# Block-recurrent cross attention and SwiGLU on one core: how weights are converted, and how batch 0 opens, dealt anew

## The chip, the core and the metric

The kernel runs on one core of a Trainium2 chip, in one launch. The metric is device time in microseconds (us). Engines are named as the profile names them: PE (TensorE; PEld are its weight loads), DVE (VectorE), ACT (ScalarE), POOL (GpSimd) and SP (SyncE), which issues most DMAs; ACT issues some.

## The reference

Eight batches of eight heads; each head has 512 tokens and 32 states of 64 features. Tokens attend to states and states to tokens; the two reads are stacked to 544 rows per batch, and the heads are laid side by side to 512 features. Then comes a feed-forward block with RMS norm and a gated hidden layer of 1536. The weights arrive as 64-bit floats, and there is no arithmetic on the host.

```python
scores = scale * np.matmul(x, state.transpose(0, 1, 3, 2))      # 512 x 32 per head
a = np.exp(scores - scores.max(-1, keepdims=True))
a /= a.sum(-1, keepdims=True) + 1e-09
xread = np.matmul(a, state)
...                                                              # a2: the same from states to tokens
sread = np.matmul(a2, x)
x = concat([xread, sread], axis=2) -> (4352, 512)
xn = x / np.sqrt(np.mean(x * x, axis=-1, keepdims=True) + 1e-06) * rms_g
g, val = xn @ w_gate, xn @ w_val                                 # 512 -> 1536
out = g * (1.0 / (1.0 + np.exp(-g))) * val @ w_out               # 1536 -> 512
```

## The kernel before

**The work.** A token's read is a mixture of states, so the gate and value weights are first multiplied with the batch's states (`own_weights`, L695, copied to SBUF at L707). A hidden product then takes the attention weights `aT_s` of the batch, scaled by each token's norm, straight to the hidden layer: `hidden` for batch 0 (products L738, Silu L744, gating L748), `hidden_seven` for the others (products L842). The output projection is `project_as_ready` for batch 0 (L945) and `project_twice` for the others (L1146). All products are in 32-bit floats.

**Stages.** Batch 0 is computed while the weights are loaded and converted, with batch 1's attention beside it. Its steps on PE, DVE, ACT, POOL and SP stand in the order that the string `ORDER` gives: every letter takes one step of one generator (`a`, `b`: the halves of batch 0's token attention; `A`: batch 1's; `s`, `S`: state reads; `e`, `d`: weight conversion on ACT and on DVE; `v`: own weights; `h`, `t`, `u`: hidden products, Silu, gating; `p`: projection; `z`: products of the identity matrix without use for the result, L1281). `FIRST` does the same for batch 1, `PERIOD` for batches 2 to 6, `LAST` for batch 7, `STATES` for the rows of the states. Each engine works through its own queue in that order.

**Weights.** A piece is 1 MB of 64-bit numbers, 128 rows by 1024. There are three for each of six pairs of hidden blocks (`mp`): 256 columns of `w_gate`, the same of `w_val`, and 256 rows of `w_out`. `load_parts` (L212) brings a piece into one of `RAW_AHEAD` = 4 buffers `raw`. `exponents` makes three passes over it on ACT (L246, L249, L252), which turn the top 16 bits into a power of two by rectifiers; `values` makes three on DVE: it masks the upper word (L273), joins the words to a mantissa (L276) and multiplies with the power (L282). The gate and value weights go to `w_m`, those of the output to `wo`; each finished `w_m` is also stored in DRAM, from where later batches fetch it.

**Batch 0's token attention.** `first_half` transposes the state rows (L463), copies them to `stT` (L466) and, with zeros between the heads, to `apart` (L468, L469). `chunk_scores` transposes 128 tokens of x at a time (L499, copied at L501) and multiplies them with `apart` (L504); maximum, difference and exponential follow (L510, L512, L514). `half_read` sums and normalizes (L522 to L527), transposes (L532, L535), multiplies with the states' Gram matrix (L539) and the weights again (L543), sums by products with ones (L548), takes the power -1/2 on POOL (`mean_root`, L299), spreads it along the rows (L306) and scales `aT_s` (L558). Each half has 256 tokens; the hidden products take all 512. `state_scores` (L568, copies L574) serves the state read.

## Time and profile before

| what | value |
|---|---|
| time before, three runs | 745.63 us median (742.44 to 745.95) |
| span of the profiled execution | 742.6 us; the page gives no time around it |
| PE busy | 735.6 us, 99% |
| DVE, ACT, POOL busy | 579.0, 380.2, 260.3 us |
| DMA | 146.15 MB, 197 GB/s over the span |
| ACT passes over a piece of 128x1024 (L246, L249, L252) | 1.25, 1.15, 1.15 us |
| DVE passes over a piece of 128x1024 (L273, L276, L282) | 0.68, 1.22, 1.22 us |

The page gives busy time by engine, a chain of work that ended last, and the costliest groups of instructions. A row of the timeline is: start in us, duration in us, engine, line, operation, what is written and read, shapes and count, and in brackets the idle time before it with what ended it. In the chain a row is start, duration, and engine with what it writes and the line. PE's records count a 32-bit product twice, as it is done in two passes.

### The profile page before, as it was taken

The page shows a single profiled execution, that of the slowest core. Times are in us where ns is not written, and L with a number is a line of the kernel's source. Part 1 is how long each engine was busy: PE and PEld are TensorE (multiplying, and loading weights), DVE is VectorE, ACT ScalarE, POOL GpSimd, SP SyncE. Part 2 cuts the span into 40 slices and gives each one's busy share as a digit, 9 for nine tenths or more (in the row PEclk, how much of TensorE's full clock was granted, in tenths as well). Part 3 has the DMA queues.
Part 4 walks back from the last instruction along what each step waited for, and adds up shares of the span by engine and source line. Part 5 has one row for each costly group of instructions (what it writes and reads, how often), then busy time and mean ns, then how long its engine had stood idle before and what let it go on. Part 6 is the DMA issues. An engine that isn't in the chain of part 4 may idle for free.

```text
span 742.6 us, 14225 instructions
## 1 busy us (share of the span) xinstructions
PE 735.6 (99%) x5582; PEld 591.0 (80%) x5582; DVE 579.0 (78%) x957; ACT 380.2 (51%) x635; POOL 260.3 (35%) x362
## 2 busy tenths in 40 slices
PE   8999999999999999999999999999999999999998
PEld 6534444779977998789878997799778987899996
DVE  4999978899856994699659985799469955798862
ACT  5999972573265725472366426562556336511220
POOL 3100004341283128512573228312841267324400
PEclk9999999999999999999999999999999999999999
DMA  9987936964783278608881669328860883063411
GB/s 296 274 294 274 398 118 223 309 245 148 239 304 105 90 285 283 195 1 297 228 304 23 226 213 315 98 95 292 274 188 6 317 230 127 1 223 117 135 52 28
DMA packets 60994, 146.15 MB, mean 197 GB/s; under 512 B 14848, under 2 KB 31744, under 8 KB 54016
## 3 DMA queue, kind: packets, MB, share of 16 engines
q1 hardware_dynamic: 47808, 125.78, 48.9%
q10 hardware_dynamic: 13120, 19.47, 9.2%
q8 instruction: 44, 0.72, 0.4%
q14 instruction: 22, 0.18, 0.1%
HBM read 116.46 MB, written 28.77 MB: 196 GB/s over the span
## 4 chain that ended last, share of the span: by engine, by line
PE 98%; ACT 1%; DMA 1%; DVE 0%; SPq 0%; issue 0%; DVEq 0%
PE f L842 40%; PE f L1146 31%; PE f L945 6%; PE pv L738 6%; PE pv L695 3%; PE at L695 3%; PE f L1008 2%; PE at L631 1%; PE at L355 1%; PE at L437 1%; DMA rows<-in_state_dram 1%; PE f L1281 0%; PE pv L504 0%; PE at L306 0%; PE at L499 0%; PE at L649 0%
## 5 line engine op out<-in xcount | busy, mean ns | idle before, releaser
L842 PE MATMUL f<-aT_s,v 128*128 128x256 f32 x504 | 118.8, 381 | 0.0
L842 PEld LDWEIGHTS f<-aT_s,v 128*128 128x128 f32 x504 | 94.8, 191 | 19.2 <-DVE h L1200 4.2
L905 DVE TENSOR_TENSOR g<-g,f 128x512 f32<-128x512 f32 x84 | 55.8, 684 | 58.6 <-PE f L842 45.7
L842 PE MATMUL f<-aT_t,vs 128*128 128x256 f32 x336 | 86.6, 381 | 0.0
L1174 POOL TENSOR_TENSOR kept<-kept 128x256 f32<-128x256 f32 x28 | 20.9, 746 | 183.2 <-DVE kept L1186 116.9
L1159 ACT COPY kept<-f 128x512 f32<-128x512 f32 (+1 forms) x56 | 30.1, 538 | 105.8 <-PE f L1146 99.8
L1146 PE MATMUL f<-w,h 128*128 128x128 f32 x588 | 74.7, 276 | 0.0
L842 PEld LDWEIGHTS f<-aT_t,vs 128*128 128x128 f32 x336 | 63.0, 190 | 12.5 <-issue 3.5
L1146 PEld LDWEIGHTS f<-w,h 128*128 128x128 f32 x588 | 69.8, 192 | 1.1 <-DVE h L1200 0.8
L722 POOL TENSOR_TENSOR vs<-v 128x256 f32<-128x256 f32 x42 | 31.0, 737 | 109.8 <-ACT v L707 109.6
L896 ACT ACTIVATE hb<-g 128x1024 f32<-128x1024 f32 x42 | 44.4, 1058 | 46.8 <-DVE g L905 43.1
L299 POOL TENSOR_TENSOR ri<-ss,mhalf 128x4 f32<-128x4 f32 (+1 forms) x9 | 9.4, 1045 | 126.9 <-issue 82.0
L918 DVE TENSOR_TENSOR hb<-hb,f 128x512 f32<-128x512 f32 (+1 forms) x48 | 31.1, 649 | 28.8 <-PE f L842 28.7
L945 PE MATMUL f<-wo,hb 128*128 128x512 f32 x96 | 44.0, 599 | 0.0
L738 PE MATMUL pv<-aT_s,v 128*128 128x512 f32 x96 | 43.8, 598 | 0.0
L842 PE MATMUL f<-aT_t,v 128*128 128x256 f32 x168 | 43.8, 383 | 0.0
L842 PE MATMUL f<-aT_s,vs 128*128 128x256 f32 x168 | 43.3, 380 | 0.0
L1146 PE MATMUL f<-wo,h 128*128 128x128 f32 x336 | 42.3, 275 | 0.0
L1146 PE MATMUL f<-wo,hb 128*128 128x128 f32 x336 | 42.1, 275 | 0.0
L918 DVE TENSOR_TENSOR hb<-hb,c 128x512 f32<-128x512 f32 (+1 forms) x48 | 35.7, 743 | 6.5 <-ACT hb L896 6.1
L1146 PEld LDWEIGHTS f<-wo,hb 128*128 128x128 f32 x336 | 40.3, 192 | 0.4
L1146 PEld LDWEIGHTS f<-wo,h 128*128 128x128 f32 x336 | 39.8, 192 | 0.0
(227 smaller groups left out, 1639.9 us busy)
## 6 DMA issues: line engine op xcount, KB each, us to landing
w_m<-w_d SPq DMA_DIRECT2D x48, 1024.0 KB
w<-t_d SPq DMA_DIRECT2D x49, 576.0 KB
out_dram<-kept SPq DMA_DIRECT2D x28, 256.0 KB
raw<-in_moe_w_val_dram SPq DMA_DIRECT2D x6, 1024.0 KB
raw<-in_moe_w_out_dram SPq DMA_DIRECT2D x6, 1024.0 KB
w_d<-w_m SPq DMA_DIRECT2D x6, 1024.0 KB
x_b<-in_x_dram SPq DMA_DIRECT2D x6, 1024.0 KB
x_d<-xB ACTq DMA_DIRECT2D x6, 1024.0 KB
```

What stands on the lines that cost most here:

```text
L695: TE.matmul(out=pv[e][Ns * j:Ns * j + Ns, :], lhsT=stT_g[b][D * e:D * e + D, j, :], rhs=w[D * e:D * e + D, j].rearrange("p m k f -> p (m k ...
L722: GE.tensor_tensor(out=vs[:, 0], in0=a21, in1=a22, op=ALU.add)
L738: TE.matmul(out=to[0], lhsT=lhs(i, k), rhs=r, start=(i == 0), stop=(i == len(rhs) - 1))
L842: TE.matmul(out=ps[:, i, 0:half], lhsT=l[:, i, :], rhs=r, start=(start and i == 0 and k == 0), stop=(k == len(lhs) - 1), skip_group_check= ...
L896: SE.activation(out=hb[:, 2 * mp:2 * mp + 2, 0:n].rearrange("p m (c t) -> p m c t", c=2), in_=q["g"][:, :, :, 0:half], func=ACTF.Silu if s ...
L905: VE.tensor_tensor(out=to, in0=to, in1=q[ps][:, :, 0:half], op=ALU.add)
L918: VE.tensor_tensor(out=part, in0=part, in1=val, op=ALU.mult)
L945: TE.matmul(out=banks[r], lhsT=hb[:, m, P * r:P * r + P], rhs=wo[:, m, :], start=(m == 0), stop=(m == NM - 1))
L1008: TE.matmul(out=banks[name][:, r, :], lhsT=lhs(k)[:, P * r:P * r + P], rhs=rhs(k), start=(start and r == 0 and k == 0), stop=(k == HM - 1) ...
L1146: TE.matmul(out=to[half][:, slot, :], lhsT=lhs[:, k, :], rhs=rhs[:, k, :], start=(fresh and n in (0, 4) and k == 0), stop=(k == QM - 1), s ...
L1159: SE.copy(of_half(k, i), banks[name][i])
L1174: GE.tensor_tensor(out=k[:, 4:8:3], in0=k[:, 5:6].to_broadcast([P, 2, QD]), in1=k[:, 4:8:3], op=ALU.add)
```

## The change

- **Conversion.** A piece lands two bytes off the start of its buffer, as 16-bit numbers, so that the 32 bits under the top 16 stand in one aligned word. ACT makes two rectifier passes (Prelu with slope 2^-20) that leave the top 16 bits as a bfloat16 number; DVE masks that to its power of two (16 bits in and out), multiplies the aligned word with it, and adds the bfloat16 number. `RAW_AHEAD` is 5. The first pair's gate and value pieces are cut by hidden block (128 columns of each) instead of by matrix.
- **Loads.** Batch 0's state rows come on ACT's queue, ahead of four rows of `rms_g`, which PE transposes. Batch 0's x comes on SP's queue in token halves (the first in two DMAs of four heads), with two neighbouring tokens side by side in runs of 512 bytes; the second half stands behind weight piece 0, and batch 1's x behind pieces 0 to 4.
- **Batch 0's attention in token halves.** One transpose covers two tokens of a head; scores use `apart` for either token. `half_read` transposes the unscaled exponentials, and one product with the Gram matrix and four columns of ones gives both the squares and the sums; the norm and the sum are then joined to one factor (with two small products and the power on POOL), the exponentials are scaled once and transposed again. The products by ones (L548), the spreading along the rows (L306) and the scaling of `aT_s` after it go.
- **Own weights and hidden products of the first pair** are made block by block (`first_own`) and by token half (`first_pair`), so that the first hidden products need half 0 and the first block alone.
- **Order.** `ORDER` and `FIRST` are written anew. The products without use take a matrix of ones set by DVE (`wake`); `z` does not occur in the new `ORDER`, and `y`, the same with other banks, occurs three times. The groups of POOL (L158, L160) move behind the opening as stream `i`; the Gram matrix and `stT_g` are a stream `g`. Memsets of `apart` and `blocks` move from POOL to DVE.
- Batch 0's token rows are stored in the new order of tokens, with as many DMAs.

```diff
-RAW_AHEAD = 4
+RAW_AHEAD = 5
 W_BUFS = 3
-FLAT = 1793.0
+FLAT = 2.0 ** 20
+ZERO = 16 * 896
...
-    "zzzaaazazbabaaabdebdbadeabeazszbbeadebeezdzbazzaabbaszeabbazzddbebeaaezbddabddsa"
+    "aaaaaaageeaaadadeeggbbigdddabbbaabgbaabgaeaaaayybydbebbvadbeeaabasvbbbvhssdbbedv"
...
+            rows[b] = x_0.tile([P, 3, D], F32, name="rows_0")
         for e in range(2):
-            nc.sync.dma_start(out=rows[b][:, e], in_=state[b, e::2])
-
-    def load_x(b, *queues):
+            (nc.sync if b else nc.scalar).dma_start(out=rows[b][:, e], in_=state[b, e::2])
...
+    def load_x_halves():
+
+        x_sb[0] = x_0.tile([P, 2, H, HT, D], F32, name="x_b")
+        for i in range(2):
+            for h in (slice(0, H // 2), slice(H // 2, H)) if i == 0 else (slice(0, H),):
+                nc.sync.dma_start(out=x_sb[0][:, i, h].rearrange("p h c d -> p h (c d)"),
+                                in_=x[0, h, HS * i:HS * i + HS, :].rearrange("h (p c) d -> p h (c d)", c=HT))
+            yield
+
+    wake = consts.tile([P, P], F32, name="wake")
+    VE.memset(wake, 1.0)
...
-    for i, bound in enumerate((-896.0 - 7.5 / 16, 1.0, 255.0 * 128, 1e-6)):
+    for i, bound in enumerate((-float(ZERO), 16.0 * ZERO / FLAT, 0.0, 1e-6)):
...
+    apart = x_0.tile([P, 2, 4, HT, Ns], F32, name="apart")
+    VE.memset(apart, 0.0)
     blocks = x_0.tile([P, P], F32, name="blocks")
-    GE.memset(blocks, 0.0)
+    VE.memset(blocks, 0.0)
+    gram = x_0.tile([P, 2, P + 4], F32, name="gram")
+    VE.memset(gram[:, :, P:P + 4], 0.0)
     for j in range(4):
-        GE.memset(blocks[Ns * j:Ns * j + Ns, Ns * j:Ns * j + Ns], 1.0 / DM)
+        VE.memset(blocks[Ns * j:Ns * j + Ns, Ns * j:Ns * j + Ns], 1.0 / DM)
+        VE.memset(gram[Ns * j:Ns * j + Ns, :, P + j:P + j + 1], 1.0)
...
+        for n in range(2):
+            if mp:
+                pieces.append([(moe_w_gate, moe_w_val)[n][:, 2 * P * mp:2 * P * mp + 2 * P]])
+            else:
+                pieces.append([dram[:, P * n:P * n + P] for dram in (moe_w_gate, moe_w_val)])
+        pieces.append([moe_w_out[2 * P * mp:2 * P * mp + 2 * P]])
...
+        raw[k] = raws.tile([P, 8 * P + 1, 4], I16, name="raw")
+        flat = raw[k].rearrange("p f four -> p (f four)")[:, 1:1 + 32 * P]
+        out_ = flat.rearrange("p (n f) -> p n f", n=len(pieces[k]))
+        for n, src in enumerate(pieces[k]):
+            nc.sync.dma_start(out=out_[:, n].rearrange("p (a f) -> p a f", a=src.shape[1]),
+                              in_=src.bitcast(I16))
...
-                ex, line = exs[k][:, columns(k, a)], lin[:, columns(k, a)]
-                half = raw[k][:, columns(k, a)].bitcast(I16)[:, :, 3::4]
-                SE.activation(out=line, in_=half, func=ACTF.Prelu, scale=1.0 / 16,
+                c = columns(k, a)
+                SE.activation(out=lin[:, c], in_=raw[k][:, c.start + 1:c.stop + 1, 0], func=ACTF.Prelu,
                               bias=bounds[:, 0:1], alpha=1.0 / FLAT)
                 yield
-                SE.activation(out=ex, in_=line, func=ACTF.Prelu, bias=bounds[:, 1:2],
-                              alpha=FLAT)
-                yield
-                SE.activation(out=ex.bitcast(U16), in_=ex, func=ACTF.Relu, scale=128.0,
-                              bias=bounds[:, 2:3])
+                SE.activation(out=tops[k][:, c], in_=lin[:, c], func=ACTF.Prelu, scale=8.0,
+                              bias=bounds[:, 1:2], alpha=FLAT)
...
+                        power_ = conv.tile([P, 8 * P], U16, name="power")
+                        words = raw[k].rearrange("p f four -> p (f four)").bitcast(U32)
+                        words = words[:, 0:16 * P].rearrange("p (f two) -> p f two", two=2)[:, :, 1]
...
-                    top, r = (t[:, columns(k, a)] for t in (top_, raw[k]))
-                    hi = r[:, :, 1]
-                    man = r.bitcast(F32)[:, :, 0]
-                    VE.tensor_scalar(top, hi, 0xfffff, 0x100000,
-                                     op0=ALU.bitwise_and, op1=ALU.bitwise_or)
+                    c = columns(k, a)
+                    top, power, rest = tops[k][:, c], power_[:, c], words[:, c].bitcast(F32)
+                    VE.tensor_scalar(power, top.bitcast(U16), 0xff80, None, op0=ALU.bitwise_and)
                     yield
-                    VE.scalar_tensor_tensor(out=man, in0=top, scalar=2.0 ** 32,
-                                            in1=r.bitcast(U32)[:, :, 0], op0=ALU.mult, op1=ALU.add)
+                    VE.scalar_tensor_tensor(out=rest, in0=words[:, c], scalar=2.0 ** -36,
+                                            in1=power.bitcast(BF16), op0=ALU.mult, op1=ALU.mult)
                     yield
-                    yield
-                    man, ex = (t.rearrange("p (a c f) -> p a c f", f=P, c=dst.shape[2])
-                               for t in (man, exs[k][:, columns(k, a)].bitcast(BF16)))
-                    VE.scalar_tensor_tensor(out=dst, in0=man, scalar=-2.0 ** -52, in1=ex,
-                                            op0=ALU.mult, op1=ALU.mult)
-                if a.stop == pieces[k].shape[1]:
+                    shape = dict(n=dst.shape[1], a=dst.shape[2], f=P)
+                    rest, top = (t.rearrange("p (n a c f) -> p n a c f", **shape)
+                                 for t in (rest, top.bitcast(BF16)))
+                    VE.tensor_tensor(out=dst, in0=rest, in1=top, op=ALU.add)
...
+        GE.tensor_copy(packed[:, 2], packed[:, 0])
+        yield
+        tp = aps.tile([P, 2, 4, Ns], F32, name="at")
+        for i in range(2):
+            TE.transpose(out=tp[:, i].rearrange("p j n -> p (j n)"),
+                         in_=packed[:, i:i + 2].rearrange("p e d -> p (e d)"), identity=ident)
+        yield
+        VE.tensor_copy(apart[0:D, :, :, 0, :], tp[0:D])
+        for e in range(2):
+            SE.copy(apart[D:P, e, :, 1, :], tp[D:P, 1 - e])
...
         yield
         yield from chunk_scores(0)
+        yield from half_read(0)
+
+    def of_states():
...
+        for j in range(0, 4, 2):
             tp = aps.tile([P, 4, P], F32, name="at")
-            for j in range(4):
-                TE.transpose(out=tp[:, j, :], in_=xb[:, c, P * j:P * j + P], identity=ident)
-            yield
-            (VE.tensor_copy if c == 1 else SE.copy)(xT[:, :, c, :], tp)
-            yield
-            for j in range(4):
-                TE.matmul(out=sc[:, c - HT * h, :, j, :], lhsT=xT[:, j, c, :], rhs=apart[:, j],
-                          start=True, stop=True)
+            for i in range(4):
+                TE.transpose(out=tp[:, i, :], identity=ident,
+                             in_=x_sb[0][:, h, 2 * j + i].rearrange("p c d -> p (c d)"))
+            yield
+            (VE.tensor_copy if h == 0 and j else SE.copy)(xT[:, h, 2 * j:2 * j + 4, :], tp)
+            yield
+        for j in range(0, 4, 2):
+            for i in range(4):
+                TE.matmul(out=sc[:, :, i % 2, j + i // 2, :], lhsT=xT[:, h, 2 * j + i, :],
+                          rhs=apart[:, i % 2, j + i // 2], start=(i == 0 and j == 0),
+                          stop=(i == 3 and j == 2), skip_group_check=True)
...
+        def transposed():
+            tp = aps.tile([P, 2, HT, P], F32, name="at")
+            for i in range(2):
+                for c in range(HT):
+                    TE.transpose(out=tp[:, i, c, :], identity=ident,
+                                 in_=eS[:, c, i].rearrange("p j n -> p (j n)"))
+            yield
+            SE.copy(aT, tp.rearrange("p e c t -> p e (c t)"))
+            yield
+
+        yield from transposed()
...
+        ge = [f.tile([P, 2, P + 4], F32, name="f") for f in (fy, fz)]
+        for c in range(HT):
+            for i in range(2):
+                TE.matmul(out=ge[c][:, i, :], lhsT=aT[:, i, P * c:P * c + P], rhs=gram[:, i, :],
+                          start=True, stop=True)
+        yield
+        sq = x_0.tile([P, HT, 2, 4, Ns], F32, name="sq_0", tag="sS")
+        for c in range(HT):
+            VE.tensor_tensor(out=sq[:, c].rearrange("p e j n -> p e (j n)"), in0=ge[c][:, :, 0:P],
+                             in1=eS[:, c].rearrange("p e j n -> p e (j n)"), op=ALU.mult)
+            yield
+        for c in range(HT):
+            VE.tensor_scalar(z[:, c].rearrange("p (e j) -> p e j", e=2), ge[c][:, :, P:P + 4],
+                             1e-9, None, op0=ALU.add)
+        VE.reciprocal(z.rearrange("p c k -> p (c k)"), z.rearrange("p c k -> p (c k)"))
+        yield
+        GE.tensor_tensor(out=z2, in0=z, in1=z, op=ALU.mult)
+        yield
+        q = two.tile([P, HT, 8], F32, name="q_0", tag="q_0")
+        VE.reduce_sum(out=q.rearrange("p c k -> p (c k)"),
+                      in_=sq.rearrange("p c e j n -> p (c e j) n"), axis=AXX)
+        yield
+        ss = two.tile([P, NC], F32, name="ss")
+        VE.tensor_tensor(out=q, in0=q, in1=z2, op=ALU.mult)
+        VE.reduce_sum(out=ss[:, 0:HT], in_=q, axis=AXX)
+        VE.tensor_scalar(ss[:, 0:HT], ss[:, 0:HT], 1e-6, None, op0=ALU.add)
+        yield
+        ri = mean_root(ss[:, 0:HT], HT)
+        GE.tensor_tensor(out=z2, in0=z, in1=ri[:, 0:HT].unsqueeze(2).to_broadcast([P, HT, 8]),
+                         op=ALU.mult)
+        yield
         e = eS.rearrange("p c e j n -> p (c e j) n")
+        VE.tensor_tensor(out=e, in0=e, in1=z2.rearrange("p c k -> p (c k)").unsqueeze(2).to_broadcast(e.shape),
                          op=ALU.mult)
         yield
+        yield from transposed()
...
+    def first_own():
+
+        w, v = w_sb[0], v_0.tile([P, 2, 2, 2, P], F32, name="v")
+        v_sb[0, 0] = v, None
+        for m in range(2):
+            pv = [(fx, aps)[m].tile([P, 2, P], F32, name=("f", "at")[m]) for e in range(2)]
+            for j in range(4):
+                for e in range(2):
+                    TE.matmul(out=pv[e][Ns * j:Ns * j + Ns],
+                              lhsT=stT_g[0][D * e:D * e + D, j, :],
+                              rhs=w[D * e:D * e + D, j, m], start=True, stop=True)
+            if m:
+                w_sb.pop(0)
+                fetch(W_BUFS)
+            yield
+            for e in range(2):
+                SE.copy(v[:, e, m], pv[e])
+                yield
...
+    def first_pair():
+
+        done_ = []
+        for m in range(2):
+            banks = [(vps, fx)[m].tile([P, S], F32, name=("pv", "f")[m]) for k in range(2)]
+            products, silu, gated = hidden(m, None, (), banks)
+            parts_0[m] = iter(()), silu, gated
+            done_.append(banks)
+        for i in range(2):
+            for m in range(2):
+                for k in range(2):
+                    for e in range(2):
+                        TE.matmul(out=done_[m][k][:, HS * i:HS * i + HS], lhsT=v_sb[0, 0][0][:, e, m, k, :],
+                                  rhs=aT_s[0][:, e, HS * i:HS * i + HS],
+                                  start=(i == 0 and e == 0), stop=(i == 1 and e == 1),
+                                  skip_group_check=True)
...
-    load_x(0, nc.scalar, nc.scalar, nc.sync, nc.sync)
+    nc.scalar.dma_start(out=rms_rows, in_=moe_rms_g.rearrange("(i p) -> i p", p=P))
+    first_x = load_x_halves()
```

## The prediction

> **What bounds the kernel now.** I read the page first, then busy time by stretch, then the chain of waits, then the first 30 us of the timeline.

> ```profile
> span 742.6 us, 14225 instructions
> PE 735.6 (99%) x5582; PEld 591.0 (80%) x5582; DVE 579.0 (78%) x957; ACT 380.2 (51%) x635; POOL 260.3 (35%) x362
> ```

> PE is the bound. The stretches show where it is not:

> ```profile
> 8.00:11.00 3.00, 3.00 (x21) 2.79 (x20) 0.06 (x1) 1.67 (x3) 0.00 (x0) 1.00 1.04 401
> 18.00:22.00 4.00, 3.45 (x20) 2.61 (x19) 3.56 (x10) 3.65 (x6) 0.00 (x0) 1.00 1.06 233
> 30.00:150.00 120.00, 120.00 (x629) 57.90 (x636) 105.63 (x153) 91.73 (x124) 17.78 (x20) 1.00 0.77 272
> ```

> The first number after the stretch is its length, the next is PE: from 30 to 150 us PE has no gap. So only two things count: when the unbroken part begins, and how much PE work it holds. (The last number is GB/s: 401 while weights land in runs of 2 KB, 233 while x lands in runs of 256 B.) The chain tells the beginning:

> ```profile
> 1.52 3.99 DMA rows<-in_state_dram
> ...
> 5.64 0.45 PE at L463
> ...
> 6.94 0.85 PE at L499 x4
> ...
> 10.46 0.44 PE at L499 x4
> ...
> 28.92 0.95 PE at L328 x8
> 29.87 5.41 PE pv L738 x12
> ```

> L738 are the first hidden products; the timeline starts them at 29.79. They need both token halves scaled (L558) and all of w_m 0 (L282), and both come late on DVE:

> ```profile
> 13.06 0.69 DVE L510 TENSOR_REDUCE m<-pv 128x16 f32<-128x512 f32 x1 [0.37 <-PE pv L504]
> 18.59 0.69 DVE L527 TENSOR_TENSOR eS<-eS,z 128x512 f32<-128x512 f32 x1
> 24.11 1.58 POOL L299 TENSOR_TENSOR ri<-ss,mhalf 128x2 f32<-128x2 f32 x1 [17.30 <-DVE ss L552]
> 25.84 1.22 DVE L282 SCALAR_TENSOR_TENSOR w_m<-raw,ex 128x1024 f32<-128x1024 f32 x1
> 28.23 1.42 DVE L558 TENSOR_TENSOR aT_s<-aT_s,pv 128x512 f32<-128x512 f32 x2
> ```

> From 13 us DVE is nearly always busy: it is the bound of the opening, and PE fills with products of the identity.

> **The start, after the change.** Three walks.

> To the first scores. The state rows landed at 5.51 behind x. On ACT's queue they go first: no later than 5.5, hardly before 3.2 (1.52 plus a third of the wait); I take 4.2, since 32 KB stand ahead instead of 512. Then POOL's copy of one row block (0.2; L158 copies 32 columns in 0.17), two transposes at the slow 0.21 each, the copies into apart (0.27 on DVE, two of 0.26 on ACT), eight transposes of x (8 x 0.21 = 1.7) while those copies run, and 16 score records at 0.17 (weight loads of L504 took 1.24 for eight at 9.08, 0.97 at 10.63). Sum 4.2 + 0.2 + 0.5 + 1.8 + 2.8 + 0.1 = 9.6 us, against 13.06. No row has x in runs of 512 B; between 233 and 401 GB/s its first half costs 1.3 to 2.2 us from about 2, and is there by 4.2 to 5.2: up to 0.8 of the 9.6 hangs on it.

> DVE, from 9.6 to half 0 scaled. Its queue holds ten passes over 512 at 0.69 (maxima and subtractions of both halves, two steps of weight piece 0a, two of 0b, the sum of squares, the scaling): 6.9. Three products of 256 at 0.42 (L1053's shape): 1.3. The Gram masks: 0.5 (L479). Three maskings of 16-bit halves: the 4-byte step L273 took 0.42 for 512 and 0.69 for 1024, these read and write half the bytes; between half of that and all of it, 0.8 to 1.5, I take 1.0. Six small ones of 0.16 to 0.25: 1.1. Sum 10.8. Where the next needs nothing of the one before it starts 0.08 early (L588: two of 0.68 in 1.27), some ten times: -0.8. POOL now stands in the chain twice: z squared (L160's 128x32 took 0.29) before the sum q is scaled, and the power L299 (0.70 and 1.58 here) with one product before the scaling. Behind the first wait stand ss and the last step of piece 0b; behind the second nothing that is ready. The 0b step, a mask and a square (1.5 together) cover most of the power: +0.4, at worst +0.9. So 9.6 + 10.4 = 20.0.

> To the first product. Four transposes 0.44, ACT's copy 0.59, hand-overs 0.15; the copy frees the bank that fifteen of the sixteen state-score products wait for (L568 took 1.02), and those stand ahead of the hidden products: 22.1 us. The first hidden products need half 0 and w_m's first block of columns alone. PE starts its unbroken part at 22.1 instead of 29.8: -7.7. If DVE were faster there, PE would be next: its own work from 9.6 is about 8.5 us at full clock (summed below).

> **PE work now behind the start.** Before, these were done by 29.8; now they follow: half of the first own weights (1.02 / 2 = 0.5), four transposes of half 1 (0.44), batch 1's state transpose (0.2) and its 16 x transposes (four times 0.44 = 1.8). Sum +2.9. The first four token products in 256 instead of 512 columns cost nothing: 0.43 for half of 0.86. The sums by ones (L548, 1.05 twice), the row broadcasts (L306) and all of z's products go, but they lay ahead of the start. The three products of ones in the new order come after the first Gram products, none before x lands.

> **New waits behind the start.** The second block of w_m is DVE's third step of piece 1, due near 24.1; PE reaches it at 23.7. Half 1's transposes wait for its scaling, and one copy of x for ACT. 0 to 1.5, I take 0.6.

> **The rest is cover.** Per piece ACT drops one of three passes (1.24 + 1.15 + 1.15 to 2.4) and DVE's first step shrinks: 18 pieces, -20 us on ACT and some -5 on DVE, with four table loads more on ACT (4 x 1.28). None is on PE's path by itself. But the cover is thin: L282 ended the third pair's weights at 54.69 and PE asked at 54.83, so weights must come as much earlier as PE now asks, about 5 us, and ACT's saving of 1.15 on each of eight pieces (9) pays for that. Batch 1's x stands behind five pieces instead of four, 2.6 us at 401 GB/s: near 25 instead of 22 to 23.5, asked for after 29. The groups on POOL (4 us) and rms_g by four rows and a transpose (0.1 on PE) are hidden; token stores and the redealt first full batch move as many bytes and products.

> **Sum.** 742.6 - 7.7 + 2.9 + 0.6 = 738.4 of span (after PE's last product at 739.0 a copy and the last stores follow, 3.6 us, as before). The median of the runs shown is 745.63, 3.0 above the profiled span (the runs went from 742.44 to 745.95); the same 4.2 off it gives 741.4. About 0.5%, 3.7 us, is what a measurement of this kernel can tell from no change, so this stands just outside it. Ends of the terms: start 21.2 (early rows, cheap masks) to 23.4, waits 0 to 1.5: -5.7 to -2.

> **Rivals.** *PE stays slow.* Four transposes took 0.85 at 6.94 and 0.44 at 10.46: PE ran at half speed until about 10 us, though the profile's clock column says 1.00, and only after long runs of identity products. The change drops these. From 9.6 to the start PE has at full speed 0.5 (Gram) + 2.3 (20 transposes) + 1.0 + 1.9 (scores, gram products) + 1.3 (ones) + 1.5 (own weights, state scores) = 8.5; at half speed 17, and the start would come at 27: 742.6 - 2.8 + 3.5 = 743.3, no change. Against it: at half speed PE has almost no gap from 4.4 on, as it had none from 5.64 to 10.4 before. If full speed comes near 14, the start is some 1.3 late and the gain 3.

> [...]

> *The weights come slower; slower than before.* Raw pieces now land two bytes off, in halves of a word, where every load in this trace lands on whole words. If that brings them from 401 GB/s to what small runs get here, 233 to 255, 1 MB takes 4.1 to 4.5 us instead of 2.6: 1.5 more for each of the eight pieces up to the third pair, 12 us, less about 8 of lead that the shorter conversion and the fifth buffer give: 4 late there. After that a pair needs 3 x 4.1 + 2.6 = 15 us of transfers while PE's pair takes 14 to 15, so it falls back further, to 12 or 14 in all: 738.4 + 13, span 751, median near 754. It decides once 1 MB costs over 3.6 us (290 GB/s). For it: DMA is already 0.77 busy from 30 to 150. Against it: runs stay 2 and 4 KB long.

> [...]

> *A longer chain.* If the 16-bit masks cost as much as the 4-byte step and POOL's power takes 1.58 each time, start and later waits lose 2 to 3 us: no change.

> **Chances.** Forecast (start between 21 and 23, weights keep up) 0.58; late clock or longer chain 0.28; slow weights 0.11; something else dear 0.03. The forecast's low end falls under 3.7 at times and a mild late clock does not always: faster 0.55, within 0.31, slower 0.14. Range: the early start and the lower of the runs shown (742.4 - 5.7) give 737; the late clock on the median (745.6 + 0.7) and the spread of the runs 747; beyond lie slow weights and a little on either side.

> **What would show it.** The first hidden product near 22 (20 to 23.5), PE without a gap over 0.5 us from 25 to 150, four transposes at 0.44 each by 11 us, ACT two passes of 1.2 per piece, the mask under 0.5, raw pieces landing 2.6 us apart. Wrong if PE waits for own weights or first products in 30 to 110 us, if pieces land over 3.6 us apart, or if the start comes after 25.

## The result, and the profile after

The changed kernel takes 756.32 us (median of four runs, 755.52 to 756.95); the kernel before, run beside it, 745.79 (742.44 to 746.54). The ratio is 1.0153, with a 95% interval of 1.0129 to 1.0177: slower by 1.5%, where 741.4 and a range of 737 to 747 stood.

The page of the changed kernel, first its lines on span and engines:

```profile
span 753.6 us, 14303 instructions
PE 735.8 (98%) x5602; PEld 594.2 (79%) x5602; DVE 577.9 (77%) x973; ACT 368.0 (49%) x626; POOL 266.4 (35%) x364
```

PE is as busy as before (735.8 us against 735.6), and the span is 11.0 longer. So PE waits more, or does later what it did earlier. Busy time by stretch (length, then PE, PEld, DVE, ACT and POOL, granted clock, DMA share, GB/s) shows where:

```profile
8.00:11.00 3.00, 2.89 (x15) 2.49 (x13) 1.11 (x2) 2.24 (x5) 1.54 (x6) 1.00 1.15 323
18.00:22.00 4.00, 4.00 (x21) 4.00 (x21) 0.99 (x2) 1.77 (x3) 0.40 (x1) 1.00 1.02 328
30.00:150.00 120.00, 119.08 (x653) 59.25 (x651) 97.69 (x146) 81.78 (x112) 23.29 (x31) 1.00 0.72 262
146.00:150.00 4.00, 3.81 (x29) 2.31 (x28) 0.69 (x1) 0.00 (x0) 0.00 (x0) 1.00 0.39 157
150.00:154.00 4.00, 0.94 (x5) 0.87 (x5) 1.49 (x3) 3.20 (x6) 0.03 (x1) 1.00 0.75 157
```

From 18 to 22 PE is now full while DVE has 0.99 of 4 us, where before DVE had 3.56: in the opening the two have changed places. From 30 to 150 PE stays covered but for 0.9. From 150 to 154 it works 0.94 of 4 us, behind a stretch in which ACT does nothing at all. The chain of waits tells the opening (start, duration, engine):

```profile
1.92 5.43 DMA rows<-in_state_dram
...
7.49 0.68 PE at L488 x2
...
10.23 3.31 PE pv L541 x16
...
16.55 1.60 PE pv L541 x8
...
19.01 1.60 PE pv L541 x8
...
26.21 0.70 DVE eS L605
...
29.43 1.92 PE pv L1354 x8
```

L1354 are the first hidden products: 29.36 in the timeline, against 29.79 before and 22.1 forecast. The state rows landed at 7.4, and the score products L541 (0.2 each) ran at half speed for both token halves.

I split each span at the first hidden product into four terms, which the experiments then take apart:

| | before | after | difference | forecast |
|---|---|---|---|---|
| first hidden product | 29.79 | 29.36 | -0.4 | -7.7 |
| gaps of PE behind it | 0.05 | 5.38 | +5.3 | +0.6 |
| PE work behind it | 709.2 | 715.2 | +6.1 | +2.9 |
| behind PE's last product | 3.6 | 3.6 | 0 | 0 |
| span | 742.6 | 753.6 | +11.0 | -4.2 |

### The profile page after: what moved, and what is told of

Read it like the earlier page. It is cut to its first block, busy times and chain, and to the rows that moved or that the text cites. A ratio compares the mean times of both kernels' runs of the same rounds, so it can differ in the third digit from the quotient of the medians.

```text
span 753.6 us, 14303 instructions
## 1 busy us (share of the span) xinstructions
PE 735.8 (98%) x5602; PEld 594.2 (79%) x5602; DVE 577.9 (77%) x973; ACT 368.0 (49%) x626; POOL 266.4 (35%) x364
## 4 chain that ended last, share of the span: by engine, by line
PE 90%; DVE 5%; DMA 2%; issue 1%; ACT 1%; ACTq 0%; POOL 0%; DVEq 0%
PE f L911 36%; PE f L1215 29%; PE f L1014 5%; PE pv L807 5%; PE pv L745 3%; PE f L1077 2%; PE at L745 2%; DMA x_d<-xB 2%; PE at L681 1%; PE at L461 1%; DVE w L1169 1%; PE pv L541 1%; PE at L379 1%; DMA rows<-in_state_dram 1%; DVE hb L1274 1%
## 5 line engine op out<-in xcount | busy, mean ns | idle before, releaser
L1243 POOL TENSOR_TENSOR kept<-kept 128x256 f32<-128x256 f32 x28 | 21.2, 756 | 202.6 <-DVE kept L1255 122.9
L757 ACT COPY v<-pv 128x512 f32<-128x512 f32 x56 | 32.0, 601 | 14.0 <-PE pv L745 6.7
```

The lines of the kernel that those rows point to most:

```text
L757: SE.copy(v[:, e].rearrange("p m k f -> p (m k f)"), pv[e])
L1243: GE.tensor_tensor(out=k[:, 4:8:3], in0=k[:, 5:6].to_broadcast([P, 2, QD]), in1=k[:, 4:8:3], op=ALU.add)
```

## The experiments

The theory after this result had three parts: the clock comes late without the products without use; the state rows come late on ACT's queue; and the new FIRST, which the prediction costed at nothing, costs most. The rivals were that DVE's chain holds the start whatever the clock, and that the weights, now two bytes off, come slower. Each ratio below is against the kernel before on the same chip. The kernel before itself had medians from 744.36 to 745.79 in these sets, so a difference between medians of two sets is good to some 1.5 us.

**The opening's products of ones, put back (a1).** The changed kernel, with

```diff
-    "aaaaaaageeaaadadeegg...
+    "zzzzzzzzaaaaaaageeaaadadeegg...
```

> The changed kernel with eight products of ones put ahead of everything else on PE, so that PE works from about 1 us until x and the state rows have landed; nothing else differs. Theory (the clock): in the changed kernel PE ran at half speed until 21.9 us although it was busy without a gap from 9.1 us on, and the first hidden product came at 29.4 instead of 22. With the products of ones full speed should come by about 10 us, as it did before the change (9.6), PE's 12.5 us of half-speed work should shrink to 6 to 8, and the first hidden product should come at 24 to 25.5: time 4 to 5.5 us under the changed kernel's 756.3, so 751 to 752. Rival (the landing of the state rows at 7.4 us and the DVE queue set the opening, the clock does not): first product still at 28 to 29.4, time 755 to 756.5.

It took 755.12 us, ratio 1.0141 (1.0121 to 1.016). The trace's record of the granted clock turns to full speed at 13.28 us instead of 21.92, and the first hidden product came at 27.93, only 1.4 earlier; the time is the rival's, not the theory's. PE's timeline shows why:

```profile
1.05 10.18 PE L1375 MATMUL f<-wake 128*128 128x256 f32 x16 [1.05 <-DVE wake L156]
11.03 0.63 PE L488 MATMUL at<-ident,rows 128*128 128x128 f32 x2
```

Eight products are too many: they hold PE until 11.2, and the state rows wait for it (in the changed kernel they had landed at 7.4). The clock came 8.6 us earlier, in the stretch in which x's transposes follow the products, and the run leaves open what an early clock is worth.

**The state rows back on SP's queue, ahead of x (a2).**

```diff
-            (nc.sync if b else nc.scalar).dma_start(out=rows[b][:, e], in_=state[b, e::2])
+            nc.sync.dma_start(out=rows[b][:, e], in_=state[b, e::2])
```

> The changed kernel with batch 0's state rows issued on SP's queue ahead of x, as before the change, instead of on ACT's queue. Theory (the second queue starves): the rows should land near 4 instead of 7.4 us, since 64 KB then stand ahead of x in one queue instead of being shared out against it. If PE's opening work at half speed is the bound, the first hidden product comes as much earlier, 3 us (26.4), and the time is 753 to 754. Rival: the release of PE's clock does not move (21.9 us), and DVE and the weights hold the first hidden product back, so that it comes at 28 to 29.4 and the time stays at 755.5 to 756.5.

It took 753.91 us, ratio 1.0128 (1.0108 to 1.0149). The first transposes of the rows start at 4.01 instead of 7.49, and the first hidden product at 27.71: 3.5 us of earlier rows bring 1.65. With the clock still late (full speed at 21.24) and the rows early, this is also the nearest test of the prediction's rival "PE stays slow", which put the start at 27. What is late next is x's second half, behind weight piece 0; the chain of waits now reads

```profile
4.27 8.11 DMA x_b<-in_x_dram
```

**The old FIRST in the changed kernel (a3).** The letters are the same in number, so the two strings can be exchanged.

> The changed kernel with the old order string for batch 1 (FIRST); the opening order and all else as changed. Theory (the redealt FIRST): the 4.2 us that PE waits between 150 and 164 us come from the new order, which puts batch 2's x store to DRAM (x_d) behind a 1 MB weight fetch, so that it took 12.8 us to land instead of 7.4. With the old order PE should wait under 1 us there: 752 to 752.8. Rival (the lateness comes from what the opening leaves to DMA and DVE): the gap stays, 755.5 to 757.

It took 749.8 us, ratio 1.0063 (1.0041 to 1.0085): 6.5 us off, more than expected, and more than half of the loss. In its profile (747.8, the lowest of the four runs) the gaps of PE behind the start fall from 5.38 to 0.75, and the PE work behind it falls from 715.2 to 712.9. The one gap left, 0.74 at 31.9, is the transposes of half 1, which wait for a copy of v on ACT.

**The kernel before without its products of the identity (b1).** All 16 letters z are taken out of its ORDER.

> The kernel before without its sixteen products of the identity (z) in the opening order. Theory (the clock): full speed comes later than 9.6 us, only when wide products follow each other, and the first hidden product comes later than 29.8 by 2 to 5 us: 748 to 751. Rival (busy PE releases the clock by itself within some microseconds of its first work at 5.6 us): the same 745.8 within 1 us.

It took 751.16 us, ratio 1.0097 (1.0068 to 1.0125). Full speed comes at 18.86, goes again from 22.27 to 25.69, and the first hidden product is at 32.56 instead of 29.79. These products are worth 6.5 us to the old kernel by the medians (744.71 beside it), and 2.8 in the start of the profiled execution, which is the fastest of the four (748.63 to 753.31).

**The repairs together (c1), and x's second half earlier (c2).** c1 has the old FIRST, the rows on SP's queue and four products of ones (`"zzzaazaaaaageeaaad`); c2 in addition

```diff
+    next(first_x)
     load_piece(0)
     next(first_x, None)
```

> The changed kernel with three corrections at once: the old FIRST, batch 0's state rows on SP's queue ahead of x, and four products of ones (three ahead of the rows' transposes, one behind them). My theory is that the three losses add: FIRST alone gave back 6.5 us of span (745.9), the rows 1.6, and an early clock makes the 24 small products before the maximum of half 0 twice as fast. Full speed by 10 to 13 us, first hidden product at 23 to 25, span 741 to 743, median 744 to 747, a tie with the kernel before. Rival: DVE's chain behind the first scores, not the clock, sets the start; then it stays at 26 to 27.5, span 744 to 745, median 747.5 to 749.

> The same as the run before it, and in addition the second half of batch 0's x is loaded ahead of weight piece 0 instead of behind it. If the second half's late landing (12.4 us with the rows on SP's queue) holds up DVE's queue, in which its maxima and subtractions stand between those of half 0, the start comes 1 to 2 us earlier than in the run before it. If the weights are what DVE waits for, it comes 1 to 2 us later, as piece 0 lands 1.3 to 2 us later. Under my theory of three additive losses alone there is no difference beyond 1 us.

c1 took 747.59 us, ratio 1.0038 (1.0022 to 1.0054), the first hidden product at 27.30; c2 746.98, ratio 1.0035 (1.0019 to 1.005), at 26.66. c1 lies on the rival's side; c2 differs from it by less than 1 us, as forecast for three additive losses. But the clock record has a reason that no theory had: full speed came early, at 6.39 and 5.12, and was taken back at 13.22 and 11.94, until 20.04 and 18.77. PE's timeline of c2 shows a pause at that place, in which ACT's two passes over weight piece 0 stand ahead of the copy of x:

```profile
9.92 0.66 PE L534 MATMUL at<-ident,x_b 128*128 128x128 f32 x4
13.50 1.97 PE L541 MATMUL pv<-apart,xT 128*128 128x64 f32 x8 [2.92 <-ACT xT L537]
```

In 11 of c1's 12 executions the mean granted clock was 0.992 to 0.995 (the time before the record's first change counts as full speed), with times from 746.16 to 749.47; the one in which it was 1.0 took 743.22.

**The new FIRST in the kernel before (b2).**

> The kernel before with the new FIRST and nothing else. My theory is that the new FIRST by itself holds the stall of 3.3 us near 150 us (the v and g copies behind a store that is issued late on ACT's queue) and about 2 us of PE work from products that no longer overlap: slower by 4 to 7 us, median 749 to 752. Rival: FIRST was written for the new opening and is harmful only behind it (with the order in which the opening leaves the buffers), then no change within 2 us here.

It took 750.58 us, ratio 1.0085 (1.0061 to 1.0108): 6.0 us slower, the mirror image of a3. FIRST is bad by itself, not only behind the new opening. Its gap of 3.25 stands there too, at 147.06. Behind it the clock was taken back for one stretch, from 148.20 to 151.61, which costs some 1.7 us (an estimate, half of the stretch); in a2 the same happened from 150.95 to 154.36, in the changed kernel's own profile not. The other part of FIRST is PE work, and one piece of that is seen in the groups by line. The reads of a batch go to two pairs of banks, at and pv, whose products run side by side in the kernel before. For 56 products of each, the second number behind the bar is the mean of one; the first is the busy sum. The kernel before, the changed one, the changed one with the old FIRST, and the old one with the new FIRST:

```profile
L437 PE MATMUL pv<-aT_s,rows 32*64 32x512 f32 x56 | 7.6, 613 | 0.0
L437 PE MATMUL at<-aT_s,rows 32*64 32x512 f32 x56 | 7.6, 613 | 0.0
```

```profile
L461 PE MATMUL pv<-aT_s,rows 32*64 32x512 f32 x56 | 8.6, 613 | 0.0
L461 PE MATMUL at<-aT_s,rows 32*64 32x512 f32 x56 | 8.5, 613 | 0.0
```

```profile
L461 PE MATMUL pv<-aT_s,rows 32*64 32x512 f32 x56 | 8.6, 612 | 0.0
L461 PE MATMUL at<-aT_s,rows 32*64 32x512 f32 x56 | 7.6, 613 | 0.0
```

```profile
L437 PE MATMUL at<-aT_s,rows 32*64 32x512 f32 x56 | 8.5, 612 | 0.0
L437 PE MATMUL pv<-aT_s,rows 32*64 32x512 f32 x56 | 7.6, 613 | 0.0
```

No product got slower; one batch's pair no longer overlaps. The 0.9 on at goes with FIRST (in the changed kernel at 201.7 us, where pv starts 0.9 behind at), the 1.0 on pv with ORDER. What held the later ones back was not traced.

**The new conversion in the kernel before (b3).** Pieces land two bytes off, with the two rectifiers, the mask, the product and the addition; the pieces stay cut by matrix.

```diff
-    VE.tensor_scalar(top, hi, 0xfffff, 0x100000, op0=ALU.bitwise_and, op1=ALU.bitwise_or)
+    VE.tensor_scalar(power, top.bitcast(U16), 0xff80, None, op0=ALU.bitwise_and)
...
-    "zzzaaazazbabaaabdebdbadeabea...
+    "zzzaaazazbabaaabebbaedddabea...
```

> The kernel before with the new conversion alone: pieces landed two bytes off, two rectifier passes on ACT, a 16-bit mask, a product and an addition on DVE; the pieces stay cut by matrix, four raw buffers, and the order of steps is the old one but for five letters that must follow the passes they read. My theory is that the conversion lies beside PE's work but for the three first steps of piece 0: no change, median within 2 us of the kernel before. Rival: raw pieces that land off a word's start come slower and PE waits for weights between 30 and 110 us; then slower by 4 to 13 us.

It took 747.03 us, ratio 1.0034 (1.0019 to 1.0049). The rival with slow weights falls: behind the opening PE has one gap of 0.92, at 103.5, and it waits there for a gating on DVE, not for weights. But 2.4 us is more than "no change within 2", and DVE's timeline shows a place for it:

```profile
14.13 0.30 DVE L273 TENSOR_SCALAR power<-ex 128x512 uint16<-128x512 uint16 x1 [1.83 <-ACT ex L250]
```

The old first step of DVE needed the raw piece alone and could run beside ACT's passes; the new one needs both passes. With that wait, and rows that landed 0.9 later in this execution, the first hidden product came at 31.38, 1.6 late. No run separates the two.

**The pause filled (d1), and the same with narrow products (d2).** d1 is c2 with five products of ones in the pause, and at the head five instead of four, which use two banks; d2 cuts each of them to two products of 64 columns.

```diff
-    "zzzaazaaaaageeaaadadeeggbbigdddabbbaabg...
+    "yyyyaayaaaaageeaaadadeeggbbzzzzigdddabzbbaabg...
```

> The run with x's second half ahead of piece 0, and in addition five products of ones in the place where PE then had nothing to do for 2.9 us (10.6 to 13.5), and the four at the head in two banks instead of one, so that they follow each other without a pause. My theory is that the clock is granted and taken back at the ends of stretches of 3.41 us, by how much PE streamed in them, and that this gap took it back until 18.8. Then full speed from 6.5 at the latest or, at an unlucky phase, from 12.5, the first hidden product at 23 to 25 instead of 26.7, and a median of 743 to 745.5, as the kernel before or a little under it. Rival: DVE's chain, which waits for weight piece 0 and ACT's two passes over it, holds the start whatever the clock; then 26 to 27 and 746 to 748.

> The same kernel with every product of ones of 256 columns replaced by two of 64 columns, which keep PE occupied for about as long (16 records of 64 columns took 3.5 us at half speed, 0.22 each, against 0.43 for a record of 256) and stream a quarter to a half as much. If the clock goes by columns streamed, it is released only at 18 to 23 us, the first hidden product comes at 28 to 31, and the median is 748 to 752. If it goes by time in which PE is occupied, there is no difference to the run with wide products (743 to 745.5).

d1 took 745.72 us, ratio 1.0017 (1.0 to 1.0035). Full speed came at 4.92 and stayed; the first hidden product is at 24.42, 5.4 before that of the kernel before, as forecast (23 to 25), and the time is still not better, since the PE work behind it is 713.3 against 709.2 and its gaps are 2.5, of which 1.26 are at 550 us, far from the opening. Against c2, which differs only in these products, the start is 2.2 earlier and the median 1.3 lower. What DVE waits for now is the conversion:

```profile
11.69 0.29 DVE L299 TENSOR_SCALAR power<-ex 128x512 uint16<-128x512 uint16 x1 [2.23 <-ACT ex L276]
11.90 0.68 DVE L550 TENSOR_TENSOR eS<-pv,m 128x512 f32<-128x512 f32 x1
```

The subtraction of half 0, ready since 9.5, stands behind the mask of piece 0. d2 took 746.43 us, ratio 1.0053 (1.0018 to 1.0088), and the median hides two groups: six executions from 745.19 to 746.92 and four from 752.56 to 756.21, where none of d1's twelve is above 748.38. The profiled one is of the first group. Its narrow products kept PE occupied without a gap through the stretch from 1.52 to 4.94, and the clock did not come; full speed came at 8.35, behind a stretch with x's eight transposes of 128 columns. So being occupied did not release the clock here, which speaks against the premise of the second expected case, and the narrow products alone did not bring it. That the release came earlier than the first case had it fits the columns of the transposes. None of the four was profiled.

**Batch 2's gathers on SP's queue (a5).** The changed kernel with

```diff
-                nc.scalar.dma_start(
+                (nc.sync if b == 2 else nc.scalar).dma_start(
```

> The changed kernel with its new FIRST, but batch 2's four gathers xG<-x_d are issued on SP's queue instead of ACT's. My theory is that the stall of 3.25 us at 153 us is the gather's issue that waits in ACT's queue for the store x_d to land (6.4 us), with the copies of v and g behind it. Then ACT goes on, that gap and the one of 0.4 behind it go, and the median falls by 3 to 4 us to 752 to 753.5; the 2 us of PE work that FIRST adds stay. Rival: the products behind it need xG itself or w_m, so that the gap only moves (to the products xG,stT or to a w_m that SP fetches late behind the waiting gather); then 755 to 757.

It took 758.04 us, ratio 1.0179 (1.015 to 1.0207), 1.7 above the changed kernel: my theory of the stall was wrong, and the rival right in kind, though its 755 to 757 was passed. Behind the gap this trace also has two stretches at half speed, from 157.69 to 164.52. ACT no longer waits, and the gap stands at the products that need the gathered x, as the wait list from 130 to 170 us has it (sum, times, longest):

```profile
PE at L379 <- DMA xG<-x_d: 3.6, 2, 3.3
```

In the changed kernel the same lateness had shown up one step earlier, at ACT, whose queue stood behind the gather's issue:

```profile
137.14 0.41 ACTq L364 DMA_DIRECT2D x_d<-xB  x1
...
150.04 0.34 ACTq L369 DMA_DIRECT2D xG<-x_d  x1
150.42 0.58 ACT L757 COPY v<-at 128x512 f32<-128x512 f32 x1 [6.38 <-DMA x_d<-xB]
```

The store is issued at 137.14, and the gather that reads it back at 150.04: 12.9 us for 1 MB, against 7.4 in the kernel before.

**One letter of FIRST moved (f1).** The first f, a fetch of 1 MB of w_m, goes from the seventh place to behind the gathers.

```diff
-    "hqahthfqqaaavvthaahthaqxuutquhhthhthhxxqthqavqhxuuaauuthtuuqqatxhq...
+    "hqahthqqaaavvthaahthaqxuutquhhthhthhxxqthqavqhxuuaauuthtuuqqaftxhq...
```

> The changed kernel; in its new FIRST one letter alone is moved: the first f, which fetches 1 MB of w_m, goes from the seventh place, ahead of batch 2's store x_d, to a place behind the four gathers that read it back (in the old FIRST the first f stands behind them too). My theory is that the store took 12.8 us instead of 7.4 because this fetch (issued 136.44, the store at 137.14) and what follows it share the transfer engines with it. Then the store lands near 145 instead of 150, the gap of 3.25 us at 153 and the small ones behind it go, and the median falls by 3 to 4 us to 752 to 753.5. Rival: the store is late because batch 2's x is issued late and SP's other stores stand in the way, and the fetch matters little: store 11 us or more, median 755 to 757; or PE then waits for the late w_m itself.

It took 752.06 us, ratio 1.0105 (1.0085 to 1.0126), 4.3 below the changed kernel by the medians and 3.6 by the two ratios. ACT's timeline:

```profile
137.98 0.41 ACTq L364 DMA_DIRECT2D x_d<-xB  x1
...
144.85 0.34 ACTq L369 DMA_DIRECT2D xG<-x_d  x1
```

6.9 us instead of 12.9, and the gap of 3.25 is gone; what is left there is one of 0.72. This settles the stall: the fetch, issued 0.7 us ahead of the store, makes it late, and whoever needs the store's data pays.

**A version that is faster than both (b4).** The kernel before, with the matrix of ones from the change for its products without use, and two more of them at the head:

```diff
+    wake = consts.tile([P, P], F32, name="wake")
+    VE.memset(wake, 1.0)
...
-            TE.matmul(out=ps, lhsT=ident, rhs=ident.unsqueeze(1).to_broadcast([P, 2, P]),
+            TE.matmul(out=ps, lhsT=wake, rhs=wake.unsqueeze(1).to_broadcast([P, 2, P]),
...
-    "zzzaaazaz...
+    "zzzzzaaazaz...
```

> The kernel before, in which the products without use take a matrix of ones set by DVE instead of the identity, so that they can start at 1.05 instead of 1.77, with two more of them at the head, so that PE has no pause until the state rows land. If the clock goes by what PE streamed in a fixed stretch of 3.41 us, it is released at 4.5 to 7.9 us in every execution, where the profile of before had 9.63 and another execution of the same opening 4.84; the first hidden product comes at 27.7 as in that one, not 29.8, and the median falls by 1 to 2 us, to 742.5 to 743.8, with fewer runs above 745. Rival: the release does not depend on it, no change.

It took 742.92 us, as expected (742.22 to 744.68 in twelve runs) beside 744.74 of the kernel before (742.16 to 748.22), ratio 0.998 (0.9966 to 0.9994). In the one profile full speed comes at 5.21; the chain of waits shows PE busy from 1.05 and the first hidden products 2.0 earlier than in the profile of before:

```profile
1.05 4.47 PE f L1283 x10
5.51 0.27 PE at L465
...
27.88 5.41 PE pv L740 x12
```

The gain is small, and it is mostly the upper half of the old spread that goes.

## Why the prediction was wrong, point by point

Two steps failed: the start, whose sum took the state rows as first and the late clock as unlikely, and the new FIRST, which was put at nothing. Either alone would have passed the range of 737 to 747: with the old FIRST put back the kernel took 749.8 (a3), and 741.4 plus FIRST's 6.5 is 747.9 (an estimate). Of the 15.2 us between the forecast span of 738.4 and the 753.6 measured, 7.3 are the start, 4.7 the gaps and 3.2 the PE work behind it.

**The start: 22.1 forecast, 29.36 measured.** Three walks gave it.

The first, to the first scores at 9.6, ended at 13.54: +3.9. Of this, 3.2 is the landing of the rows. I took 4.2 and "no later than 5.5", since 32 KB stood ahead of them instead of 512; they landed at 7.36, 5.4 us after their issue, while x and the raw pieces went through SP's queue. That a queue of their own makes them first was an assumption, and no row of the trace bore on it; a2 shows them at 4.0 on the queue ahead of x, while in a3, f1 and a5, where they stay on ACT's queue, their transposes start at 7.85 to 8.65. Why that queue is later was not traced. It is also the mis-sized bound: I gave it an upper end that the old place had, as if a move could not make it worse.

The second, DVE's chain, was summed at 10.4 and took 13.4 (13.54 to 26.91). The durations were right: the three maskings took 0.28, 0.29 and 0.42, 0.99 in all where 1.0 stood, and the power 1.08. What the sum left out is a wait in the middle:

```profile
16.91 0.69 DVE L301 SCALAR_TENSOR_TENSOR raw<-raw,power 128x512 f32<-128x512 uint32 x1
20.64 0.69 DVE L548 TENSOR_REDUCE m<-pv 128x16 f32<-128x512 f32 x1 [3.05 <-PE pv L541]
21.70 0.42 DVE L581 TENSOR_TENSOR sq<-f,eS 128x256 f32<-128x256 f32 x1 [0.36 <-PE f L576]
```

The maximum of half 1 stands in DVE's queue ahead of half 0's square, and PE made its scores at half speed until 20.6. A chain was summed along one engine that also waits for the other. The third walk, 2.1, took 2.45.

**The late clock was a rival, and it was the case.** It stood at 27 for the start, 743.3 and, with the longer chain, 0.28. The place is right: until 21.9 PE ran everything at half speed. The argument against it was the step that failed: "at half speed PE has almost no gap". PE had none from 9.12 to 21.6, as said, and the clock still came only at 21.92. That a PE without a gap gets full speed early was my estimate; no run shows it, and this one speaks against it. What the traces show is that every change of the granted clock lies on a grid of 3.413 us (5.12, 11.94 and 18.77 in c2), and that full speed followed 18 of the 19 stretches of that grid in which PE had streamed 1536 columns or more (last section). In the kernel before, the products that bring the clock are worth 6.5 us (b1). In the changed kernel with the old FIRST, the clock, the rows and the place of x's second half are worth 4.1 together (749.8 in a3, 745.72 in d1; 3.4 by the ratios). Of this, keeping the clock through the pause is 1.3 (c2 to d1); the rest was not separated. With both repaired, d1 still starts at 24.42 and not at 22.1, as DVE waits for the conversion (under Cover below).

**FIRST: "move as many bytes and products".** That is true, and it was costed at nothing; it cost 6.5 us (a3), 6.0 the other way (b2). The unit of cost was wrong: with equal bytes, a fetch that is issued 0.7 us ahead of a store which PE's next products hang on is worth 3.6 to 4.3 us (f1). The rest is small waits and PE work. The PE work behind the start is 2.3 us less in a3's profile than in the changed kernel's: 0.9 is the pair of products that lost its overlap, and 1.4 was not traced. The place of the letter f against the store behind it can be read in the string, so this could have been a rival; it was none.

**PE work behind the start.** +2.9 forecast, +3.8 with the old FIRST. The 2.9 and the 1.0 of the pv pair, which no longer runs beside at, would give that; the 2.9 was not measured by itself.

**New waits.** 0.6 forecast (0 to 1.5). Without FIRST's they were 0.75 (a3), nearly all at half 1's transposes, as named, but behind ACT's copy of v and not behind their scaling.

**Cover.** The conversion stayed hidden from 30 to 150, as forecast, and the raw pieces in runs of 2 KB came nearly as fast as before (185 to 199 packets per us, some 390 GB/s, against 186 to 204); the rival with slow weights did not occur. "Runs stay 2 and 4 KB long" was not so for the first pair: cut by hidden block, its gate and value pieces come in runs of 1 KB, at some 345 GB/s (337 packets in the us from 11). What the cover argument missed is order: the first pass of DVE over a piece now follows both passes of ACT. In the changed kernel this was hidden by the late scores; with these early it costs DVE 2.2 us (d1).

**The chances.** Slower had 0.14, most of it (0.11) for one mechanism that did not occur; "something else dear", which FIRST was, had 0.03. The forecast summed one opening and took the other 700 us as unchanged, although the second string was as new as the first.

## What to carry to other kernels

A schedule that is written anew costs something even with the same bytes and products: look at what is issued just ahead of each store that is read back, and at which products lose a partner they ran beside. Before products "without use" are removed, look at what the ones that remain stream, not at whether the engine has a gap: PE had none from 9.12 to 21.6 in the changed kernel, and full speed came at 21.92; products of 64 columns alone did not bring it in d2 (1.52 to 4.94). A wait can also be followed by a stretch or two at half speed: 3.41 us in b2, behind a gap of 3.25, and in a2; 6.83 in a5, behind one of 3.3; none in the profile of the changed kernel. And a chain on one engine is only as short as the sum of its own work if nothing in its queue waits for the other half of the data.

## What the runs showed of the clock

| columns in a stretch at half speed | stretches | full speed at its end |
|---|---|---|
| under 1000 | 26 | 0 |
| 1000 to 1412 | 24 | 0 |
| 1536 | 4 | 3 |
| 1538 and more | 15 | 15 |

So the clock was released by a stretch that was about three quarters full, not by one without a pause. The table leaves out four stretches in which products over 64 rows by 32 columns run side by side (16 records of 256 columns took 0.66 us at 21.11 of d1, where eight of 128 by 128 took 1.99 at 24.42), so that the count passes 2048. Three were followed by full speed; the fourth, in a5 from 157.69, was not. If each product is weighted by the part that it fills of the 128 by 128 of the widest records (64 by 32 is an eighth), and by the part of it that lies in the stretch, the fourth has only 1278, and all 73 stretches fall into place: none up to 1440 released the clock, each from 1488 on did.

Score products of 64 columns occupied PE for 0.22 a record and filled half of that, and the opening of the changed kernel gave 1344, 1216 and 1412 columns in the three stretches from 8.3 to 18.5. The first ones of a1 followed each other every 0.64 us instead of 0.43 and gave 1280: eight of them in a row did not bring the clock. Writing one bank is not what slows them, since b4's ten records, all into one tile, took 0.45 each; in a1 each product takes the pool's one buffer as a new tile, and that this costs the time was not tested by itself. At full speed, where 4096 fit, it was taken back at the end of each of the six stretches with 512 to 1348 columns (1348 in c2) and kept with 1536 and more. The counts are worked out from the records of products, of which some can be missing, and no run measured the limit by itself.
